# A gated scan with an expert for the top 128 rows: a re-planned instruction order, a rank counted on ScalarE from a second product, and fewer spare products

## The chip, the cores and the metric

The kernel runs on one core of one Trainium2 chip. The metric is the device time of one execution in microseconds; the median of three runs of the kernel before is 204.53 us (204.34 to 205.04).

## What is computed

Four sequences of 6208 tokens with 256 features go through a gated recurrence, and after it 128 tokens of each sequence go through a small expert network. In the reference, cut to what matters:

```python
sig = 1.0 / (1.0 + np.exp(-f_logit))
f = lower_bound + (1.0 - lower_bound) * sig
for t in range(S):                       # S = 6208
    h = f[:, t] * h + (1.0 - f[:, t]) * x[:, t]
    y[:, t] = h
...
scores = np.einsum('bsd,d->bs', y, w_gate)
for b in range(B):                       # B = 4
    top_idx = np.argpartition(-scores[b], capacity)[:capacity]   # capacity = 128
    xe = y[b, top_idx]
    ye = np.maximum(xe @ w1, 0.0) @ w2   # 256 -> 1024 -> 256
    g = 1.0 / (1.0 + np.exp(-scores[b, top_idx]))
    out[b, top_idx] = xe + g[:, None] * ye
```

All inputs and outputs are float32.

## The kernel before, in words

**Units.** The four sequences are cut into 25 units of at most 1024 tokens (UNITS, L27), six or seven to a sequence (a batch, in the code's words). Features lie on the partitions, in two halves. A unit is loaded as its gate logits and its x, each 1 MB, either by two transfers (L390) or, where two neighbouring buffers are free, by one of 2 MB (L393). ScalarE makes the gate (L396) and from it the factor of the scan (L400). POOL scales x (L404) and weighs it by the gate (L408); a share of the columns (SHARE, L28) is weighed by VectorE instead (L417). VectorE scans each half (L420). TensorE makes the scores of the tokens (L429) and turns the result so that tokens lie on the partitions (L373); ScalarE, or for the units in EASED (L29) VectorE, copies the turned blocks back (L444), and SP's queue stores the unit (L447). All buffers of a unit come from 22 slots of one tile, whole.

**Search.** When a sequence is scanned, choose() finds its 128 best tokens. The scores are spread over 32 lanes (L515), each lane gives its 16 best (L525 to L531, places by L527 and L540), 14 of these per lane are laid out as a row of 448 candidates, which one product broadcasts to all partitions (row(), L546, into the PSUM tile acc), and each partition ranks four candidates of its own against that row: it counts how many are greater. A rank is a counting pass of VectorE (L563), or, for the numbers in SIGNED, a sum of signs on ScalarE (L560, settled at L568). From each rank a 0/1 mark is made (L576) on POOL or VectorE, and four small products with the marks (pull(), L580) put the chosen token numbers in order on the partitions. The searches of batches 0 to 2 work in acc, one PSUM bank; that of batch 3 (RUSH) keeps its lanes in score, another bank, and its row in acc. A flag product (tell(), L593) follows, which says whether the result is complete.

**Expert.** POOL gathers the 128 rows from the output in HBM (fetch(), L650), so it comes after the stores that wrote them. TensorE turns the gathered rows (L674; L678 for batch 3), makes the up products (L720; L711), ScalarE the ReLU (L728), TensorE the down products (L733; L738), VectorE the sum with the gate (L745; L742), and POOL scatters the rows back (L749). For batches 0 and 1 the last two units are held: they stay in their slots, their stores come last of all in SP's queue, and the search's rows in them are picked by products. A tiny copy on POOL ("passed", L789) stands between the first held store and the other three, which wait for it in SP's queue. In batch 3 POOL touches each stored unit of that batch first (see(), L635), which makes it wait for the unit's store.

**What sets the order.** Nothing is left to a scheduler: a class Plan takes all steps with their costs and what they depend on, places them on the engines one by one, and the instructions are emitted in that order. The tables at the top of the file (SHARE, EASED, CAPS, SINGLE, FIND, EXPERT, EXTRA and others) are its settings: which unit takes which path, how far ahead loads go, when a search or an expert may start. Each engine then works through its own list in order, so whatever stands behind a waiting instruction waits too. SP's queue holds all loads and stores in one order. In gaps of TensorE the plan puts spare products (L962), and at the end L958, whose results nobody reads.

For a step that works in a search bank the plan keeps two times of that bank: a reader waits for the last writer, and a writer for the last reader.

Of the kernel before, what the change touches and what calls it, by code (L numbers as in the profile page):

```python
# [19 lines left out]
P = 128  # L20
# [7 lines left out]
SHARE = [2, 1, 1.75, 0.25, 0.5, 0, 0.5, 1, 0.375, 0.125, 1, 0.125, 0, 1, 0, 0, 1, 0.25, 1, 0.375, 0, 0.875, 0.875, 0.125, 0]  # L28
EASED = [0, 1, 2, 4, 6, 8, 9, 10, 15, 16, 18, 22, 23]  # L29
SLOTS = {"big": 22, "pt": 2, "gt": 2}  # L30
SCRATCH = 1024
CAPS = {"x": 30, "f": 3, "y": 17}
SINGLE = [2, 5, 8, 11, 17, 18, 24]
PAIR, PATIENCE, LONE = 4.915, 0, -2.5
APART = [2]
RUSH = [3]
SIGNED = [[], [2, 3], [2, 3], []]
XFER, FIRST = 2.485, 2.4
AHEAD, BACKLOG, STORE = 5, 4, 450
TURN, PUT, FIND, EXPERT = 22, 1, [-570, -1350, -705, -4710], [-85, -1920, -1020, -440]  # L40
WEIGHTS_AT = 8
EXTRA = [140, 140, 180, -120, 40, -160, 100, -160, -200, -120, -200, 120, 60, 0, -80, 80, -100, -140, 120, 0, 200, -140, 60, -40, -60]
# [6 lines left out]
KEEP, SPARE, SLACK, WAKE, COLD = 0.9, 0.11, 0.1, 2.0, 5.2  # L49
# [10 lines left out]
HEADS = -620  # L60
# [13 lines left out]
class Plan:  # L74
# [23 lines left out]
    def run(self):  # L98
# [17 lines left out]
        wrote, read = {}, {}  # L116
# [15 lines left out]
        def can(i):  # L132
            when = ready[i]
            for name, writes in self.bank[i]:
                when = max(when, (read if writes else wrote).get(name, 0.0))
# [26 lines left out]
        for done in range(n):  # L162
# [77 lines left out]
            for name, writes in self.bank[i]:  # L240
                last = wrote if writes else read
                last[name] = max(last.get(name, 0.0), end + HOP)
# [28 lines left out]
def gated_scan_moe(tc, xf, heads_in, lbwg, w12, outs, cap):  # L271
    nc = tc.nc
    v, a, pe, g = nc.vector, nc.scalar, nc.tensor, nc.gpsimd
    with ExitStack() as ctx:
# [214 lines left out]
        def choose(b):  # L489
# [8 lines left out]
            def chain(eng, cost, fn, key=None, extra=(), after=None, over=None, bank=()):  # L498
                key = key or ("search", b, len(plan.ops))
                add(eng, cost, fn, p0 + 0.01 * len(plan.ops), [after or last[0], *extra], key, load=2.0 if eng == "pe" else 1.0, over=over, bank=bank)  # L500
                last[0] = key
                return key
# [6 lines left out]
            bank = score[:, 1 - b % 2] if rush else acc  # L509
            own0 = NPOS + OWN if rush else A_OWN  # L510
# [36 lines left out]

            def own(what):
# [8 lines left out]
            def ranks(k):  # L557
                if k in SIGNED[b]:
                    junk = new("junks", [P, ROW], BF16)
                    a.activation(junk, acc[:, :ROW], ACTF.Sign, scale=-1.0, bias=st["mine"][:, k : k + 1], accum_out=st["sign"][:, k : k + 1])  # L560
# [12 lines left out]
            def marks(k):  # L573
                if k == 0:
                    st["hot"] = new("hot", [P, OWN, P], BF16)
                (v if rush and k in (SIGNED[b] or [OWN - 1]) else g).tensor_scalar(st["hot"][:, k], slot, st["rank"][:, k : k + 1], None, ALU.is_equal)  # L576
# [38 lines left out]
            ranked, s = [], r  # L615
# [408 lines left out]
```

## Time and profile before

| | us |
|---|---|
| median of 3 runs | 204.53 |
| lowest, highest | 204.34, 205.04 |
| the profiled execution | 204.95 |
| its span, first to last instruction | 202.8 |

| engine | busy us (share of the span) |
|---|---|
| TensorE products | 188.8 (93%) |
| VectorE | 160.8 (79%) |
| ScalarE | 154.3 (76%) |
| POOL | 150.4 (74%) |

The transfers move 79.64 MB, at 393 GB/s over the span. The span is what the profile's timelines cover; the execution's own time is a little more than 2 us longer. A share of busy time is a mean over the whole span: what limits a stretch is read from that stretch, in the windows, and from the waits ahead of an instruction, which a timeline row gives in square brackets with what ended them. TensorE's busy time contains the spare products.

### The profile page before, as it was taken

The numbers are of one execution on the slowest core, as the hardware profiler recorded it, in microseconds if no ns is written. First come the engines' busy times: TensorE is split into PE (matmuls) and PEld (weight loads), VectorE is DVE, ScalarE is ACT, GpSimd is POOL, SyncE is SP. The second block draws the span as 40 slices with busy tenths as digits, with TensorE's granted clock in tenths as the row PEclk, the third lists the DMA queues.
The fourth block names the chain that finished last, engine by engine and source line by source line (L and its number), as shares of the span: only waits on it lengthen the run. The fifth ranks groups of instructions, "written<-read, shape, count | busy, mean of one in ns | idle before, by whom it ended". The sixth has DMA issues, their size and how long they took to land. (4 is left out here: it accounts for less than half of the span.)

```text
span 202.8 us, 4152 instructions
## 1 busy us (share of the span) xinstructions
PE 188.8 (93%) x1613; PEld 138.8 (68%) x1613; DVE 160.8 (79%) x195; ACT 154.3 (76%) x201; POOL 150.4 (74%) x143
## 2 busy tenths in 40 slices
PE   5899999989898899999999999999999998999990
PEld 3677788666665677775975667766975756759890
DVE  1859896995999889999869899999999959591210
ACT  3788898798786995889999999986979988612210
POOL 6152899995776999997999998599868997233231
PEclk9999999999999999999999999999999999999997
DMA  6999999999999999999999999999999999996941
GB/s 198 402 434 436 409 399 434 417 419 436 422 422 419 417 441 423 425 430 430 422 415 425 423 402 375 300 445 414 436 419 415 423 430 427 420 420 247 430 175 36
DMA packets 9655, 79.64 MB, mean 393 GB/s; under 512 B 1313, under 2 KB 1581, under 8 KB 2720
## 3 DMA queue, kind: packets, MB, share of 16 engines
q1 hardware_dynamic: 9104, 78.39, 93.3%
q0 software_dynamic: 384, 0.95, 1.4%
q8 instruction: 14, 0.23, 0.4%
q14 instruction: 9, 0.07, 0.1%
q10 hardware_dynamic: 144, 0.00, 0.0%
HBM read 53.48 MB, written 25.95 MB: 392 GB/s over the span
## 5 line engine op out<-in xcount | busy, mean ns | idle before, releaser
L420 DVE TENSOR_TENSOR_SCAN whole<-gt,whole 128x1024 f32<-128x1024 f32 (+1 forms) x42 | 96.6, 2314 | 2.3 <-POOL whole L408 1.0
L408 POOL TENSOR_TENSOR whole<-whole 128x1024 f32<-128x1024 f32 (+6 forms) x41 | 84.8, 2084 | 6.8 <-ACT whole L396 5.5
L373 PEld LDWEIGHTS pt<-ident,whole 128*128 128x128 f32 x384 | 48.3, 196 | 21.9 <-ACT whole L444 10.4
L373 PE MATMUL pt<-ident,whole 128*128 128x128 f32 x384 | 59.8, 293 | 2.4 <-ACT whole L444 2.3
L400 ACT ACTIVATE gt<-whole,nl 128x1024 f32<-128x1024 f32 (+2 forms) x50 | 54.6, 1097 | 6.8 <-DVE whole L420 5.5
L404 POOL TENSOR_SCALAR whole<-whole,nl 128x1024 f32<-128x1024 f32 (+6 forms) x41 | 41.0, 1011 | 19.0 <-DMA whole<-xf 13.6
L444 ACT COPY whole<-pt 128x512 f32<-128x512 f32 (+1 forms) x86 | 47.3, 590 | 8.3 <-PE pt L373 7.1
L396 ACT ACTIVATE whole<-whole 128x2048 f32<-128x2048 f32 (+2 forms) x25 | 46.3, 1855 | 6.2 <-DMA whole<-xf 6.0
L962 PE MATMUL score<-slot,ones 128*128 128x256 bf16 x356 | 48.2, 282 | 2.4 <-POOL slot L305 1.9
L962 PEld LDWEIGHTS <-ones 128*128 128x128 bf16 x356 | 35.4, 102 | 10.0 <-issue 4.0
L429 PE MATMUL score<-whole,wgr 128*32 128x256 f32 x384 | 32.3, 391 | 1.4 <-DVE whole L420 0.9
L417 DVE SCALAR_TENSOR_TENSOR whole<-gt,whole 128x1024 f32<-128x1024 f32 (+6 forms) x19 | 15.5, 818 | 8.8 <-ACT gt L400 8.7
L420 DVE TENSOR_TENSOR_SCAN whole<-gt,tl,whole 128x1024 f32<-128x1024 f32 (+1 forms) x8 | 15.3, 1933 | 0.1
L429 PEld LDWEIGHTS score<-whole,wgr 128*32 128x32 f32 x384 | 8.2, 108 | 9.2 <-DVE whole L420 3.4
L666 PE MATMUL acc<-whole,hT 128*128 128x256 f32 x64 | 14.5, 379 | 0.0
L576 POOL TENSOR_SCALAR hot<-slot,rank 128x128 bf16<-128x128 bf16 x15 | 9.0, 607 | 6.1 <-DVE vals L571 5.4
L666 PEld LDWEIGHTS acc<-whole,hT 128*128 128x128 f32 x64 | 11.9, 190 | 1.4
L720 PE MATMUL pm<-xT,wt 128*128 128x128 f32 x96 | 11.8, 279 | 0.0
L720 PEld LDWEIGHTS pm<-xT,wt 128*128 128x128 f32 x96 | 11.1, 192 | 0.5 <-ACT xT L691 0.5
L749 POOL DMA_INDIRECT out<-res,aim x4 | 4.1, 1034 | 9.5 <-DVE xT L684 4.6
L728 ACT ACTIVATE hT<-pm 128x512 f32<-128x512 f32 x8 | 4.7, 590 | 6.0 <-PE pm L711 2.4
L563 DVE TENSOR_SCALAR_CACHE_REDUCE junk<-acc,mine 128x448 bf16<-128x448 f32 x12 | 8.1, 678 | 1.2 <-ACT junks L560 0.8
(124 smaller groups left out, 131.9 us busy)
## 6 DMA issues: line engine op xcount, KB each, us to landing
whole<-xf SPq DMA_DIRECT2D x16, 2048.0 KB, 18.3
out<-whole SPq DMA_DIRECT2D x23, 1024.0 KB, 14.2
whole<-xf SPq DMA_DIRECT2D x14, 1024.0 KB, 21.8
wt<-w SPq DMA_DIRECT2D x1, 2048.0 KB, 25.5
whole<-xf SPq DMA_DIRECT2D x2, 768.0 KB, 7.7
out<-whole SPq DMA_DIRECT2D x1, 768.0 KB, 12.6
tl<-heads SPq DMA_DIRECT2D x1, 512.0 KB, 3.7
whole<-xf SPq DMA_DIRECT2D x2, 256.0 KB, 4.1
```

Source lines behind the costliest of these rows:

```text
L373: pe.transpose(out, src, ident)
L396: a.activation(fs[i], fs[i], ACTF.Sigmoid, scale=-1.0)
L400: a.activation(gs[i, h][:, :n], fs[i][:, h], ACTF.Identity, scale=nl[:, h : h + 1], bias=1.0)
L404: g.tensor_scalar(xs[i][:, h, c0:], xs[i][:, h, c0:], nl[:, h : h + 1], 1.0, ALU.mult, ALU.mult)
L408: g.tensor_tensor(xs[i][:, h, c0:], xs[i][:, h, c0:], fs[i][:, h, c0:], ALU.mult)
L417: v.scalar_tensor_tensor(xs[i][:, h, :c1], gs[i, h][:, :c1], 1.0, xs[i][:, h, :c1], ALU.subtract, ALU.mult)
L420: v.tensor_tensor_scan(xs[i][:, h], gs[i, h][:, :n], xs[i][:, h], carry[h] if blk0 else tl[:, 1, h, b, TAIL - 1 : TAIL], ALU.mult, ALU.add ...
L429: pe.matmul(score[j * CG : (j + 1) * CG, b % 2, c0:], wgr[:, h, CG - 1 - r : 2 * CG - 1 - r], src, start=(h == 0 and blk0 + q < 3), stop=( ...
L444: (v.tensor_copy if eng == "dve" else a.copy)(out, src)
L666: pe.matmul(acc[:, :D], st["hits"][:, c], yms[last_unit[b] - k][:, c], start=(k == 0 and c == 0), stop=(k == HELD[b] - 1 and c == NF - 1))
L720: pe.matmul(st["pm", f // TP][:, c : c + P], w1t[:, h, f * P : (f + 1) * P], st["xT"][:, h], start=(h == 0), stop=(h == NH - 1))
L962: pe.matmul(score[:, h].rearrange("p (k c) -> p k c", k=2), ones, slot.unsqueeze(1).to_broadcast([P, 2, P]), start=not begun, stop=True, s ...
```

## The change

The change has four parts.

1. **The plan's account of a search bank.** Of each bank the plan now keeps, per engine, the time of its last access of either kind, and a step waits for every other engine's last access; an engine's own earlier steps don't hold it up.
2. **The last search.** SIGNED for batch 3 becomes [3]: the fourth rank is counted by ScalarE, not VectorE. It reads a second copy of the row of candidates, made by a second product (row_aside) into a PSUM buffer of the class gt, so another bank. The marks of the last two ranks are made on VectorE (swift), those of the first two on POOL. In batch 1 one rank less is ScalarE's.
3. **"passed" moves.** The tiny copy that releases three of the held stores now comes ahead of batch 3's gather, which depends on it; before, it came behind.
4. **The tables.** KEEP goes from 0.9 to 0.8 and SLACK from 0.1 to 0.2, which govern the spare products (306 are emitted, 356 before), and all other settings of the plan are replaced. So every engine's list is in another order.

Of the tables two lines stand for all:

```diff
-EASED = [0, 1, 2, 4, 6, 8, 9, 10, 15, 16, 18, 22, 23]
+EASED = [1, 3, 4, 5, 14, 21, 23, 24]
-SIGNED = [[], [2, 3], [2, 3], []]
+SIGNED = [[], [3], [2, 3], [3]]
...
-KEEP, SPARE, SLACK, WAKE, COLD = 0.9, 0.11, 0.1, 2.0, 5.2
+KEEP, SPARE, SLACK, WAKE, COLD = 0.8, 0.11, 0.2, 2.0, 5.2
...
-        wrote, read = {}, {}
+        touched = {}
...
-                when = max(when, (read if writes else wrote).get(name, 0.0))
+                when = max([when, *(t for who, t in touched.get(name, {}).items() if who != self.ops[i][0])])
...
             for name, writes in self.bank[i]:
-                last = wrote if writes else read
-                last[name] = max(last.get(name, 0.0), end + HOP)
+                touched.setdefault(name, {})[e] = end + HOP
...
+            swift = [OWN - 2, OWN - 1] if rush and SIGNED[b] else [OWN - 1] if rush else []
...
+            def row_aside():
+                st["aside"] = hold(("aside",), [P, 4 * BLK], "aside")
+                pe.matmul(st["aside"][:, :ROW], onesf[:LANE], st["diag"].rearrange("p l e -> p (l e)"), start=True, stop=True)
...
-                    a.activation(junk, acc[:, :ROW], ACTF.Sign, scale=-1.0, bias=st["mine"][:, k : k + 1], accum_out=st["sign"][:, k : k + 1])
+                    a.activation(junk, (st["aside"] if rush else acc)[:, :ROW], ACTF.Sign, scale=-1.0, bias=st["mine"][:, k : k + 1], accum_out=st["sign"][:, k : k + 1])
...
-                (v if rush and k in (SIGNED[b] or [OWN - 1]) else g).tensor_scalar(st["hot"][:, k], slot, st["rank"][:, k : k + 1], None, ALU.is_equal)
+                (v if k in swift else g).tensor_scalar(st["hot"][:, k], slot, st["rank"][:, k : k + 1], None, ALU.is_equal)
...
-            ranked, s = [], r
+            s = r
+            if rush and SIGNED[b]:
+                s = chain("pe", 1.01, row_aside, after=r, over=0.09, takes=[("aside",)])
+                plan.tile(("aside",), ("gt", "gt"), [("aside", "read")])
             for k in range(OWN):
                 if k in SIGNED[b]:
-                    s = chain("act", 0.74, lambda k=k: ranks(k), after=s, extra=[m], bank="acc r")
+                    s = chain("act", 0.74, lambda k=k: ranks(k), ("aside", "read") if rush else None, after=s, extra=[m], bank=() if rush else "acc r")
                     continue
                 r = chain("dve", 0.65, lambda k=k: ranks(k), after=r, extra=[m], bank="acc r")
-                quick = rush and not SIGNED[b] and k == OWN - 1
+                quick = k in swift
                 marked.append(chain("dve" if quick else "pool", 0.25 if quick else 0.605, lambda k=k: marks(k), after=r))
             if SIGNED[b]:
-                r = chain("act", 0.2 * len(SIGNED[b]), settle, after=s, extra=[r])
-                marked += [chain("dve" if rush else "pool", 0.25 if rush else 0.605, lambda k=k: marks(k), after=r) for k in SIGNED[b]]
+                r = chain("act", 0.2 * len(SIGNED[b]), settle, after=s, extra=[] if rush else [r])
+                marked += [chain("dve" if k in swift else "pool", 0.25 if k in swift else 0.605, lambda k=k: marks(k), after=r) for k in SIGNED[b]]
...
-            add("pool", 1.1, fetch, p0, [("st", b), ("index", b), ("seen", N - 2) if halved else None, ("store", last_unit[b] - HELD[b]), ("store", "tail", b)], k("fetch"))
+            ahead = [("st", b), ("index", b), ("seen", N - 2) if halved else None, ("store", last_unit[b] - HELD[b]), ("store", "tail", b)]
+            if halved and len(stored) > len(unheld) + 1:
+                first = stored[len(unheld) + 1]
+                add("pool", 0.12, lambda: g.tensor_copy(yms[first][:1, 0, :1], yms[first][:1, 0, :1]), p0, ahead, ("passed",))
+                ahead = [*ahead, ("passed",)]
+            add("pool", 1.1, fetch, p0, ahead, k("fetch"))
...
-                if len(stored) > len(unheld) + 1:
-                    first = stored[len(unheld) + 1]
-                    add("pool", 0.12, lambda: g.tensor_copy(yms[first][:1, 0, :1], yms[first][:1, 0, :1]), p0 - 2, [k("fetch")], ("passed",))
```

POOL at the end of the program, before: the copy of the indices of batch 3, the six touches of stored units (L635), the gather of batch 3 (xe_109 is the tile that takes its rows) and the tiny copy "passed" (L789).

```order
L638 COPY index<-idx 128x1 [waits DVE_49]
L635 MEMSET whole 1x1 [waits DMAHW0_49]
L635 MEMSET tl 1x1 [waits DMAHW3_49,Pool_49]
L635 MEMSET whole 1x1 [waits DMAHW1_49]
L635 MEMSET whole 1x1 [waits DMAHW2_49]
L635 MEMSET whole 1x1 [waits DMAHW3_49]
L635 MEMSET whole 1x1 [waits DMAHW4_49,Activation_49]
L650 DMA xe_109<-out,idx 128x256 [waits DMAHW5_49]
L789 COPY whole<-whole 1x1
L749 DMA out<-res,aim 6208x256 [waits DMASW2_49,DVE_49]
```

The same place in the new order, with the numbers of the new file:

```order
L645 COPY index<-idx 128x1 [waits DVE_49]
L642 MEMSET whole 1x1 [waits DMAHW1_49]
L642 MEMSET tl 1x1 [waits Pool_49]
L642 MEMSET whole 1x1 [waits DMAHW2_49]
L642 MEMSET whole 1x1 [waits DMAHW3_49]
L642 MEMSET whole 1x1 [waits DMAHW4_49]
L642 MEMSET whole 1x1 [waits DMAHW5_49,Activation_49]
L779 COPY whole<-whole 1x1
L657 DMA xe_109<-out,idx 128x256 [waits DMAHW6_49]
L756 DMA out<-res,aim 6208x256 [waits DMASW2_49,DVE_49]
```

The tiny copy (now L779) stands ahead of the gather and has no wait of its own; the wait for the store of the last unit (a DMAHW semaphore) stands on the gather alone.

TensorE from the last of the four products of batch 3's pull (L580) on, before: L720 and L733 are batch 2's up and down products, L593 is the flag, L678 turns the rows of batch 3's gather (xe_109). Four more up products of batch 2 (L720, x4) stand ahead of the pull.

```order
L580 LDWEIGHTS hot
L580 MATMUL acc<-vals,hot 128x3
L720 MATMUL pm<-xT,wt 128x128 x4
L593 LDWEIGHTS ones
L593 MATMUL acc<-bad,ones 128x1
L720 MATMUL pm<-xT,wt 128x128 x8
L733 MATMUL py<-wt,hT 128x256 x8
L678 MATMUL pm<-ident,xe_109 128x128 x2
```

And now, with the numbers of the new file (L584 is the pull, L967 a spare product, L597 the flag, L727 and L740 are the up and down products):

```order
L584 LDWEIGHTS hot
L584 MATMUL acc<-vals,hot 128x3
L967 LDWEIGHTS ones
L967 MATMUL warm<-slot,ones 128x512
L597 LDWEIGHTS ones
L597 MATMUL acc<-bad,ones 128x1
L727 MATMUL pm<-xT,wt 128x128 x16
L740 MATMUL py<-wt,hT 128x256 x8
L967 LDWEIGHTS ones
L967 MATMUL warm<-slot,ones 128x512
```

All 16 up products of batch 2 stand behind the pull and the flag now. Behind the last row shown come two more spare products, and then the turn of batch 3's rows (L685).

VectorE in the search of batch 3, before, from the places of each lane's second eight to the pulled number (L563 are the ranks, L700 is the gate product of batch 2's expert, L576 a mark):

```order
L540 MAX_INDEX at<-ci,rest 32x8
L543 CAST ci<-at 32x16
L563 TENSOR_SCALAR junk,rank<-acc,mine 128x448
L571 TENSOR_SCALAR vals<-score 128x4
L563 TENSOR_SCALAR junk,rank<-acc,mine 128x448 x2
L700 SCALAR_TENSOR_TENSOR res,gate<-xe_107,wgrow 128x256
L563 TENSOR_SCALAR junk,rank<-acc,mine 128x448
L576 TENSOR_SCALAR hot<-slot,rank 128x128
L585 TENSOR_REDUCE idx<-acc 128x1
```

And now (L443 is the copy of a turned block, L567 a rank, L580 a mark, L707 the gate product):

```order
L540 MAX_INDEX at<-ci,rest 32x8
L443 COPY whole<-pt 128x4x128
L543 CAST ci<-at 32x16
L567 TENSOR_SCALAR junk,rank<-acc,mine 128x448 x2
L575 TENSOR_SCALAR vals<-score 128x4
L567 TENSOR_SCALAR junk,rank<-acc,mine 128x448
L580 TENSOR_SCALAR hot<-slot,rank 128x128 x2
L707 SCALAR_TENSOR_TENSOR res,gate<-xe_107,wgrow 128x256
L589 TENSOR_REDUCE idx<-acc 128x1
```

One rank has gone, a copy has come in ahead of the ranks, a second mark has come, and the gate product stands behind the marks.

## Rows read from the trace of the kernel before

**Rows 1.** The page's first line.

```profile
span 202.8 us, 4152 instructions
```

**Rows 2.** Windows: stretch us, each engine's busy us (instructions), granted clock, DMA share, GB/s.

```profile
120.00:125.00 5.00, 4.82 (x49) 3.31 (x48) 4.90 (x9) 5.00 (x9) 4.23 (x6) 1.00 1.01 387
...
125.00:130.00 5.00, 4.96 (x44) 3.80 (x43) 4.75 (x7) 5.00 (x10) 4.57 (x4) 1.00 1.02 326
...
175.00:180.00 5.00, 4.94 (x51) 2.62 (x50) 3.45 (x15) 1.66 (x3) 0.01 (x1) 1.00 1.00 415
...
184.50:185.00 0.50, 0.50 (x7) 0.50 (x7) 0.00 (x0) 0.00 (x0) 0.50 (x1) 1.00 0.16 66
```

**Rows 3.** Timeline of VectorE: start us, us, engine, line, what [idle before].

```profile
170.81 2.35 DVE L420 TENSOR_TENSOR_SCAN whole<-gt,whole 128x1024 f32<-128x1024 f32 x1 [0.30 <-ACT gt L400]
...
179.19 0.68 DVE L563 TENSOR_SCALAR_CACHE_REDUCE junk<-acc,mine 128x448 bf16<-128x448 f32 x1 [0.32 <-PE acc L546]
...
181.25 0.42 DVE L700 SCALAR_TENSOR_TENSOR res<-xe,wgrow 128x256 f32<-128x256 f32 x1
...
181.60 0.68 DVE L563 TENSOR_SCALAR_CACHE_REDUCE junk<-acc,mine 128x448 bf16<-128x448 f32 x1
...
182.32 0.25 DVE L576 TENSOR_SCALAR hot<-slot,rank 128x128 bf16<-128x128 bf16 x1
...
182.93 0.15 DVE L590 TENSOR_SCALAR bad<-acc 128x1 bf16<-128x1 f32 x1
```

**Rows 4.** Timeline of TensorE, products and the last weight load.

```profile
179.16 1.47 PE L958 MATMUL warm<-slot,ones 128*128 128x512 bf16 x6
...
181.31 1.16 PE L720 MATMUL pm<-xT,wt 128*128 128x128 f32 x8
...
182.34 0.47 PE L580 MATMUL acc<-vals,hot 128*128 128x3 bf16 x4
...
183.68 2.03 PE L720 MATMUL pm<-xT,wt 128*128 128x128 f32 x16
...
185.54 3.62 PE L733 MATMUL py<-wt,hT 128*128 128x256 f32 x16
...
188.78 0.36 PEld L678 LDWEIGHTS pm<-ident,xe 128*128 128x128 f32 x2
```

**Rows 5.** Timeline of POOL.

```profile
184.15 1.11 POOL L650 DMA_INDIRECT xe<-out,idx  x1 [0.52 <-issue]
...
185.26 0.18 POOL L789 COPY whole<-whole 1x1 f32<-1x1 f32 x1
...
198.06 0.99 POOL L749 DMA_INDIRECT out<-res,aim  x1 [1.51 <-POOLq L874]
```

**Rows 6.** Line L650, gathers of batches 1, 2 and 3: issue to landing.

```profile
DMA to landing us min/median/max: 8.9/8.9/8.9
DMA to landing us min/median/max: 6.6/6.6/6.6
DMA to landing us min/median/max: 3.3/3.3/3.3
```

**Rows 7.** Groups by line and form: times, busy us, mean ns.

```profile
L417 DVE SCALAR_TENSOR_TENSOR whole<-gt,whole 128x1024 f32<-128x1024 f32 x6 | 7.3, 1218 | 2.9 <-ACT gt L400 2.9
...
L444 DVE COPY whole<-pt 128x512 f32<-128x512 f32 x11 | 7.4, 674 | 0.2 <-PE pt L373 0.2
```

**Rows 8.** Waits: engine, line, waited for, us in total, times, longest.

```profile
DVE mine L555 <- PE acc L546: 1.3, 1, 1.3
...
DVE junk L563 <- ACT junks L560: 0.8, 1, 0.8
```

**Rows 9.** Line L447, the store of batch 3's last unit.

```profile
L447 SPq DMA_DIRECT2D out<-whole x1: 332/332/332, 177.3 to 177.3; - x1
...
DMA to landing us min/median/max: 6.2/6.2/6.2
```

**Rows 10.** Line L962, the spare products.

```profile
L962 PE MATMUL score<-slot,ones x356: 269/273/421, 1.9 to 169.4; 128*128 128x256 bf16 x178
```

More of the change, by code (lines that the diff above doesn't have):

```diff
@@ L27 @@
 UNITS = [[1, 3, 4, 4, 4, 4, 4], [4] * 6, [4] * 6, [4] * 6]
-SHARE = [2, 1, 1.75, 0.25, 0.5, 0, 0.5, 1, 0.375, 0.125, 1, 0.125, 0, 1, 0, 0, 1, 0.25, 1, 0.375, 0, 0.875, 0.875, 0.125, 0]
-EASED = [0, 1, 2, 4, 6, 8, 9, 10, 15, 16, 18, 22, 23]
+SHARE = [2, 2, 1.625, 0, 0.875, 0.625, 0.875, 0, 0.625, 0, 1, 0.5, 0.375, 1, 0.125, 0, 0.25, 0.875, 0.375, 1, 1, 0, 0.875, 0.375, 0.5]
+EASED = [1, 3, 4, 5, 14, 21, 23, 24]
 SLOTS = {"big": 22, "pt": 2, "gt": 2}
 SCRATCH = 1024
-CAPS = {"x": 30, "f": 3, "y": 17}
-SINGLE = [2, 5, 8, 11, 17, 18, 24]
-PAIR, PATIENCE, LONE = 4.915, 0, -2.5
+CAPS = {"x": 33, "f": 3, "y": 21}
+SINGLE = [2, 10, 11, 13, 16, 18, 19, 21]
+PAIR, PATIENCE, LONE = 4.915, 8.5, 10.5
 APART = [2]
 RUSH = [3]
-SIGNED = [[], [2, 3], [2, 3], []]
+SIGNED = [[], [3], [2, 3], [3]]
 XFER, FIRST = 2.485, 2.4
[L39 to L42, printed above, removed]
+AHEAD, BACKLOG, STORE = 15, 3, 320
+TURN, PUT, FIND, EXPERT = 12, -13, [-3450, -405, -4655, -8840], [-1005, -2245, -985, 175]
+WEIGHTS_AT = 6
+EXTRA = [-60, 200, -40, -100, 200, -200, -60, 60, 120, 200, -60, -80, 0, 60, 40, -80, -200, 80, -80, 0, -140, 160, -20, 140, 80]
 AFTER = "pull"
@@ L59 @@
 HALF = 2048
-HEADS = -620
+HEADS = -860
 NROW = NBLK // 4 + 1
@@ L496, in choose, with chain @@
             last = [None]
-            def chain(eng, cost, fn, key=None, extra=(), after=None, over=None, bank=()):
+            def chain(eng, cost, fn, key=None, extra=(), after=None, over=None, bank=(), takes=()):
                 key = key or ("search", b, len(plan.ops))
-                add(eng, cost, fn, p0 + 0.01 * len(plan.ops), [after or last[0], *extra], key, load=2.0 if eng == "pe" else 1.0, over=over, bank=bank)
+                add(eng, cost, fn, p0 + 0.01 * len(plan.ops), [after or last[0], *extra], key, load=2.0 if eng == "pe" else 1.0, over=over, bank=bank, takes=takes)
                 last[0] = key
```

## The prediction

> **What bounds the kernel now.** The page's first line gives the span of the profiled execution, 202.8 us [rows 1]; the execution itself took 204.95 us, so 2.15 us lie around the span. The median of the runs shown is 204.53, that is 0.42 below the profiled one. I make the sum against 204.95 and take 0.42 off at the end. Read next the windows [rows 2]: in the last third the share of the DMA engines stays at 1.0 (387, 326 and 415 GB/s) and VectorE is busy for 4.90 and 4.75 of 5 us. So until the last scan two things are full, the queue of transfers and VectorE. In 184.50 to 185.00 the share is 0.16: here the queue runs dry before its stores are done.
>
> From VectorE's timeline [rows 3] take the anchor S: the last scan starts at 170.81, lasts 2.35 and ends at S = 173.16. Behind S stands a chain. The search of batch 3 makes its ranks (179.19 to 182.32) and the marks, and TensorE pulls the indices out, from 182.34 for 0.47, done at 182.81 [rows 4]. Then TensorE does the rest of batch 2's expert, up to 185.71 and down from 185.54 for 3.62, and only then, at 188.78, it turns the rows of batch 3's gather. POOL issued that gather at 184.15 [rows 5], and it landed 3.3 us later [rows 6], at 187.4. So the gather waited 1.3 us for TensorE. From 188.78 to the end of the span are 14.0 us, the expert of batch 3, its scatter and the landing; the change leaves these steps as they are. The question is when TensorE takes up that turn (T, now 188.78): it needs its own queue done and the gather landed.
>
> **The change part by part.** *The order up to S.* SP's order has before the last load the same 10 MB of unit stores as now, only other ones, and one tail store more (64 KB, under 0.2 us at 415 GB/s). So the last load lands where it does now, and nothing that moves among loads and stores gives time at the end. On VectorE I count what stands between the first maximum of batch 1's search and the last scan, in both orders: one rank more (0.68 [rows 3]), eight products for seven, with 768 elements more (1.22 per 1024 [rows 7], so 0.9), two copies of turned blocks fewer (0.67 each [rows 7]); together +0.3. Against that stand the stalls of the searches in the shared bank, 1.3 and 0.8 us in the search of batch 2 [rows 8]: the new plan counts a bank as taken by one engine at a time, so it can put other work there. All of it gone gives S = 171.4, none gone 173.5; an estimate for the search of batch 1 is that 0.8 more goes there, the size of the smaller of the two, so 170.6 is the early end. I take S = 171.9, since VectorE needs its rows in order behind ScalarE and POOL in any plan and I see no reason for either end. That is 1.3 us early.
>
> *The search of batch 3.* The fourth rank leaves VectorE: its 0.72 (181.60 to 182.32 [rows 3]) go. The gate product of batch 2, which starts at 181.25 and holds the fourth rank up by 0.35, moves behind the marks: another 0.35. One mark more runs on VectorE, 0.25. In its place a copy of a turned block (0.67 [rows 7]) stands ahead of the first rank, which had 0.32 us of idle time to give [rows 3], so +0.35. The second row product (its twin took 1.01 us of TensorE) and ScalarE's count lie beside VectorE's three ranks; if that cover were gone, the third mark would wait up to 1.0 us. Sum -0.5: the pull is done at S + 9.15 instead of S + 9.65, that is at 181.05.
>
> *TensorE between the pull and T.* Now 5.97 us (182.81 to 188.78). In the new order the first quarter of batch 2's up products no longer stands ahead of the pull, and nothing but a spare product fills the wait for the flag. So behind the pull come: the flag's inputs and its product, 0.65 (VectorE ends the flag's input at 183.08, 0.27 after the pull [rows 3], and the product with its hops follows); the up products, 1.16 for the first 8 of 32 passes, as much for the next 8 and 2.03 for the last 16 [rows 4], 4.35; the down products 3.62; three spare products, 0.25 each by the six in 1.47 [rows 4], 0.74. That is 9.36, or 3.4 us more. TensorE is free at 181.05 + 9.36 = 190.4, which is S + 18.5. What cost nothing before, because the wait for the flag was filled, is now on the path.
>
> *The gather of batch 3.* It reads rows that the stores of batch 3 write, so POOL waits for the last of them. That store is issued at 177.3 and lands 6.2 us later [rows 9], at 183.5. The new queue has the same bytes ahead of it, so it lands at 183.5 again, and the gather starts at about 183.7, 0.45 earlier than now; a faster search cannot pull it further. So the whole gain of the search ends at this landing. More important is what lies beside the gather. Now the tiny copy that releases the last three held stores stands behind it (185.26, after 184.15 [rows 5]), and the queue is nearly empty meanwhile (0.16 [rows 2]). In the new order that copy stands ahead of it and does not wait for the last store, so the three stores are in the queue before the gather is. A gather into the idle queue took 3.3 us to land, the two into a full one shown took 6.6 and 8.9 [rows 6]. I take 6.6, because it also ran beside 1 MB stores: 183.7 + 6.6 = 190.3.
>
> The Trainium skill ("DMA: Bandwidth & Descriptors", on queues, rings and completion order) says that each DMA engine goes round the queues packet by packet and empties a packet of some 9 to 17 descriptors before it changes over. That speaks against this edit, and the rows agree with it in sign: 3.3 us more in a full queue. An estimate from that page: 9 to 17 packets of 8 KB ahead on each of 16 engines, at the measured 415 GB/s 0.31 us each, are 2.8 to 5.3 us on top of 3.3, so the gather would land at 189.8 to 192.3 and T would be 190.4 to 192.3, against the 190.4 that the rows give.
>
> *The rest.* The held stores now run on without the gap, so they end earlier by that stretch; the scatters that wait for them are off the path, since the last scatter (198.06) stood 1.51 us idle for the mix [rows 5]. Nothing is gained there.
>
> **The sum.** T is the later of 190.4 (TensorE) and 190.3 (gather): 190.4, or 1.6 us later than 188.78. The span becomes 204.4, the profiled execution 206.55, and less 0.42 this is 206.1 us. Two causes that don't depend on each other give nearly the same T, so either alone is enough.
>
> **Rivals.** *Faster: the queue runs ahead.* From 120 to 130 us it moved 387 and 326 GB/s at a full share [rows 2], against 415 later. At 415 the same bytes are through 1.4 us earlier. If that slow stretch doesn't return in the new order, the last store lands at 182.1 and the gather, still beside stores, at 188.9; S, which follows the loads, can come to its early end less 1.4, 169.2, and TensorE is free at 169.2 + 18.5 = 187.7. With the gather then a little better than 6.6, at 5.5 (between the ends), T is 187.8, 1.0 us early: 203.5. It decides from T < 188.2. For it: the slow rows lie where one gather (the one of 8.9) ran, and that gather moves. Against it: three gains must meet.
>
> *No change: the queues interleave.* If the gather's transfers are taken in turn with the stores', it hardly feels them. By the 3.3 of [rows 6] the gather then lands at 187.0, and TensorE alone sets T: with S at 170.6, 170.6 + 18.5 = 189.1, 0.3 late, 204.8. Against it stand the 6.6 and 8.9. The Trainium skill says in the same page (issuing engines are not separate DMA queues) that the transfers of all issuing engines interleave on the same 16 DMA engines, which speaks for it.
>
> *That it doesn't do what it says*: ScalarE's count could wait for the second product and end behind VectorE's third rank; then the search keeps its length, the pull is at S + 9.65 and T at 190.9, 206.6. Within the forecast's range.
>
> *Slower still: TensorE's clock.* It is granted 1.00 in all these windows [rows 2], the upper of its two levels (2.4 GHz). The spare products that fill its gaps fall from 356 [rows 10] to 306. If a gap now lets the grant fall to 1.2 GHz before the experts, the products between pull and T (7.97 of the 9.36 us) slow down in that stretch. No row holds a product at the lower level, so I bound it by the ratio of the two: a quarter of them at twice the time is 2 us, 208.1.
>
> **How the numbers follow.** Forecast, T between 189.5 and 191.5 (205.2 to 207.2): 0.52. Faster rival: 0.27, since nearly every edit of the order can also shorten waits that I don't see. Interleaved or in between, T within 0.6 of now: 0.15. Clock or S at its late end (173.5, so T = 192.0, 207.7): 0.06. About 0.3% (0.6 us) is what a measurement of this kernel can tell from no change. So faster 0.27, same 0.15, slower 0.58. The range is 203.4 (the faster rival) to 207.3 (the forecast's late end); outside it I leave the clock and a deeper gain.
>
> **What would show it.** In the new profile the last scan should end near 171.9, the pull near 181.0, the gather should start near 183.7 with the DMA share at 1.0 beside it and land near 190.3; TensorE should go from the flag through 32 up and 16 down products without a stop and turn batch 3's rows at 190.4. If the gather lands under 4 us after its start, the term of the full queue was wrong. If TensorE stands idle before the turn by more than 1 us, S came earlier than I took it and the gather alone sets the time. If the last store of batch 3 lands before 182, the queue ran ahead, and the faster rival holds.

## The result, and the profile after

The changed kernel takes 207.57 us (median of four runs, 207.37 to 208.07), the kernel before beside it 204.78. The ratio is 1.011, with a 95% interval of 1.007 to 1.015: slower, as forecast. The forecast was 206.1 in a range of 203.4 to 207.3. Applied to the 204.53 from which it was made, the ratio gives 206.8, inside the range; the median of 207.57 itself lies 0.3 above its upper end. The profiled execution took 207.37, where the sum had 206.55. Every ratio here and below leaves out executions that lie over 1.5% above the fastest of the same kernel.

The span, which answers to [rows 1]:

```profile
span 205.5 us, 4047 instructions
```

The windows of the changed kernel, with the columns of [rows 2] (each engine's busy us, granted clock, DMA share, GB/s):

```profile
120.00:125.00 5.00, 4.60 (x42) 2.96 (x39) 4.80 (x4) 5.00 (x7) 4.79 (x4) 1.00 1.05 418
125.00:130.00 5.00, 5.00 (x34) 3.88 (x31) 4.90 (x3) 4.75 (x6) 4.92 (x4) 1.00 0.97 407
...
185.00:190.00 5.00, 0.31 (x2) 0.00 (x0) 0.26 (x1) 0.00 (x0) 1.03 (x1) 1.00 0.96 395
190.00:195.00 5.00, 4.89 (x27) 4.45 (x28) 0.69 (x4) 1.03 (x3) 1.70 (x2) 0.66 0.18 66
```

Three things are new. The slow stretch of the queue (387 and 326 GB/s in [rows 2]) is not there. From 185 to 190 no engine works for more than 1.03 us while the queue is nearly full: everything waits for a transfer. And from 190 to 195 TensorE is granted only 0.66 of its clock on average (by single us 0.50 from 191 to 193, the lower of its two levels, 1.2 GHz, and 1.00 again from 194).

VectorE (start us, us, engine, line, what), which answers to [rows 3]:

```profile
163.71 4.58 DVE L419 TENSOR_TENSOR_SCAN whole<-gt,whole 128x1024 f32<-128x1024 f32 x2
...
176.37 0.41 DVE L580 TENSOR_SCALAR hot<-slot,rank 128x128 bf16<-128x128 bf16 x2
```

The last scan ends at 163.71 + 4.58 = 168.29, 4.9 us earlier than the 173.16 of before, and 3.6 earlier than forecast. At the first maximum of batch 1's search 2.3 of these 4.9 us are there already; the two rows are of the kernel before and of the changed one:

```profile
106.34 0.36 DVE L525 MAX8 ci<-acc 32x8 f32<-32x194 f32 x1 [1.58 <-PE acc L515]
```

```profile
104.04 0.35 DVE L525 MAX8 ci<-acc 32x8 f32<-32x194 f32 x1 [1.20 <-PE acc L515]
```

TensorE, which answers to [rows 4]:

```profile
176.50 0.54 PE L584 MATMUL acc<-vals,hot 128*128 128x3 bf16 x4
...
177.39 3.82 PE L727 MATMUL pm<-xT,wt 128*128 128x128 f32 x32
181.04 3.62 PE L740 MATMUL py<-wt,hT 128*128 128x256 f32 x16
184.50 0.81 PE L967 MATMUL warm<-slot,ones 128*128 128x512 bf16 x3
190.11 0.41 PE L685 MATMUL pm<-ident,xe 128*128 128x128 f32 x2 [4.81 <-DMA xe<-out,idx]
...
190.82 5.31 PE L718 MATMUL pm<-xT,wt 128*128 128x128 f32 x32
```

TensorE has done all of batch 2 at 185.31 and then stands idle for 4.81 us, for the gather. It turns batch 3's rows at 190.11 (forecast 190.4), and the 32 up products behind that take 5.31 us, where the same 32 took 3.84 in the kernel before. POOL, and the time of its gather, which answer to [rows 5, 6]:

```profile
179.86 0.17 POOL L779 COPY whole<-whole 1x1 f32<-1x1 f32 x1
182.56 1.10 POOL L657 DMA_INDIRECT xe<-out,idx  x1 [2.52 <-DMA out<-whole]
...
DMA to landing us min/median/max: 7.4/7.4/7.4
```

The tiny copy lets the held stores go at 179.86. The gather waits until 182.56 for the last store of batch 3 and lands 7.4 us later, at 190.0, instead of 3.3.

### The profile page after: what moved, and what is told of

It reads as the page before. It is cut to its first block, busy times and chain, and to the rows that moved or that the text cites. A ratio compares the mean times of both kernels' runs of the same rounds, so it can differ in the third digit from the quotient of the medians.

```text
span 205.5 us, 4047 instructions
## 1 busy us (share of the span) xinstructions
PE 183.3 (89%) x1561; PEld 136.8 (67%) x1561; DVE 161.0 (78%) x194; ACT 155.8 (76%) x205; POOL 142.0 (69%) x142
## 5 line engine op out<-in xcount | busy, mean ns | idle before, releaser
L407 POOL TENSOR_TENSOR whole<-whole 128x1024 f32<-128x1024 f32 (+6 forms) x41 | 79.3, 1949 | 8.0 <-ACT whole L395 7.7
L372 PE MATMUL pt<-ident,whole 128*128 128x128 f32 x384 | 58.8, 291 | 3.5 <-ACT whole L443 2.9
L443 ACT COPY whole<-pt 128x512 f32<-128x512 f32 (+1 forms) x90 | 49.2, 588 | 9.6 <-PE pt L372 9.5
L403 POOL TENSOR_SCALAR whole<-whole,nl 128x1024 f32<-128x1024 f32 (+6 forms) x41 | 38.8, 954 | 21.8 <-DMA whole<-xf 21.7
L971 PE MATMUL score<-slot,ones 128*128 128x256 bf16 x306 | 41.0, 284 | 1.9 <-POOL slot L304 1.9
L971 PEld LDWEIGHTS <-ones 128*128 128x128 bf16 x306 | 30.8, 102 | 8.1 <-issue 2.5
L428 PE MATMUL score<-whole,wgr 128*32 128x256 f32 x384 | 31.3, 390 | 4.8 <-DVE whole L419 4.0
L416 DVE SCALAR_TENSOR_TENSOR whole<-gt,whole 128x1024 f32<-128x1024 f32 (+7 forms) x21 | 18.4, 875 | 3.7 <-ACT gt L399 3.7
L428 PEld LDWEIGHTS score<-whole,wgr 128*32 128x32 f32 x384 | 8.8, 108 | 13.4 <-DVE whole L419 7.8
L580 POOL TENSOR_SCALAR hot<-slot,rank 128x128 bf16<-128x128 bf16 x14 | 8.4, 605 | 5.6 <-DVE junk L567 5.4
L727 PE MATMUL pm<-xT,wt 128*128 128x128 f32 x96 | 11.5, 278 | 0.0
L727 PEld LDWEIGHTS pm<-xT,wt 128*128 128x128 f32 x96 | 11.0, 192 | 0.4 <-ACT open L711 0.4
L567 DVE TENSOR_SCALAR_CACHE_REDUCE junk<-acc,mine 128x448 bf16<-128x448 f32 x12 | 8.0, 665 | 0.2 <-PE acc L546 0.2
```

The costliest lines, as they stand in the source:

```text
L372: pe.transpose(out, src, ident)
L403: g.tensor_scalar(xs[i][:, h, c0:], xs[i][:, h, c0:], nl[:, h : h + 1], 1.0, ALU.mult, ALU.mult)
L407: g.tensor_tensor(xs[i][:, h, c0:], xs[i][:, h, c0:], fs[i][:, h, c0:], ALU.mult)
L416: v.scalar_tensor_tensor(xs[i][:, h, :c1], gs[i, h][:, :c1], 1.0, xs[i][:, h, :c1], ALU.subtract, ALU.mult)
L428: pe.matmul(score[j * CG : (j + 1) * CG, b % 2, c0:], wgr[:, h, CG - 1 - r : 2 * CG - 1 - r], src, start=(h == 0 and blk0 + q < 3), stop=( ...
L443: (v.tensor_copy if eng == "dve" else a.copy)(out, src)
```

## The experiments

Each run starts from the kernel before or from the changed kernel and names what differs. The kernel before took 204.5 to 204.6 us beside all of them.

### The gather and the copy

**The changed kernel with the copy behind the gather again** (after_gather_first). On POOL two instructions change places, and TensorE has one spare product less ahead of the turn of batch 3's rows; all other lists are the same. POOL's list, in short:

```diff
-L779 COPY whole<-whole 1x1
 L657 DMA xe<-out,idx 128x256
+L796 COPY whole<-whole 1x1
```

> The changed kernel with only its third part undone: the tiny copy that releases three held stores stands behind batch 3's gather again; the lists of all engines are otherwise those of the changed kernel. Theory 1 (the gather was late because the released stores were in the queue beside it, and the expert behind it then ran at a lower clock): the gather starts at 182.6 as now but lands 3.3 us later instead of 7.4, at about 185.9; TensorE, free at 185.3, waits less than 1 us instead of 4.8, keeps its clock at 1.00, and the 32 up products take 3.84 us instead of 5.31. That is 4.0 + 1.5 us less than 207.57: 202.1 (201.5 to 203.0), below both kernels. Theory 2 (the gather's 7.4 us belong to the place and time of the gather in the new order, not to the copy): the landing stays near 190 and the time at 207.4. Theory 3 (the gain is given back, because the held stores then end later and their scatters set the end): gather at 185.9, but the end stays above 204.

203.63 us, ratio to the kernel before 0.994 (0.991 to 0.997); so 3.9 us less than the changed kernel, from one exchanged pair of instructions. The first profile fence is TensorE's timeline, the second POOL's with the gather's time to landing:

```profile
186.19 0.41 PE L685 MATMUL pm<-ident,xe 128*128 128x128 f32 x2 [0.34 <-DMA xe<-out,idx]
...
186.90 3.84 PE L718 MATMUL pm<-xT,wt 128*128 128x128 f32 x32
```

```profile
183.08 1.10 POOL L657 DMA_INDIRECT xe<-out,idx  x1 [2.61 <-DMA out<-whole]
184.19 0.18 POOL L796 COPY whole<-whole 1x1 f32<-1x1 f32 x1
...
196.30 0.98 POOL L756 DMA_INDIRECT out<-res,aim  x1 [5.60 <-DMA out<-whole]
197.59 0.99 POOL L756 DMA_INDIRECT out<-res,aim  x1 [0.30 <-DMA out<-res,aim]
...
DMA to landing us min/median/max: 3.0/3.0/3.0
```

Theory 1 holds for the gather (3.0 us), the wait (0.34) and the up products (3.84 again). Theory 3 holds for a part: the expected 202.1 was missed by 1.5 us. From the turn to the end of the span are 15.6 us, not 14.0 as before. The rows of POOL say why: a scatter at 196.30 waited 5.60 us for a held store, and batch 3's scatter, whose rows were ready at 194.76, stood behind it.

**That, with batch 3's scatter ahead of batch 1's** (gather_first_scatters_swapped). Of the line that gives a scatter its conditions only the last one changes, which is shown here:

```diff
-*([("moe", c, "scatter") for c in range(b) if HELD[c]] if halved else [])
+*([("moe", 0, "scatter")] if halved else [("moe", B - 1, "scatter")] if b == 1 else [])
```

> The run after_gather_first with one more edit: on POOL the scatter of batch 3 stands ahead of the scatter of batch 1, which waits for the last held store; all other lists are the same. In the trace of after_gather_first batch 1's scatter starts at 196.30, 0.8 after the last held store landed, and batch 3's, whose rows are mixed at 194.76, stands behind it and starts at 197.59. Theory 1 (part of the gain is given back at the end, because the scatters stand in POOL's list behind the held stores): batch 3's scatter starts 0.5 after its mix, at 195.3, batch 1's at 196.6, and the end comes 1.0 us earlier: 202.6 (202.0 to 203.2). Theory 2 (the end hangs on the landing of the held stores alone, or the two scatters only change places): 203.6.

202.22 us, ratio 0.9875 (0.985 to 0.990). POOL's two last scatters:

```profile
194.88 0.98 POOL L756 DMA_INDIRECT out<-res,aim  x1 [4.33 <-DVE res L749]
196.18 1.00 POOL L756 DMA_INDIRECT out<-res,aim  x1 [0.30 <-issue]
```

Batch 3's scatter now follows its own mix, and the last one starts 1.4 us earlier; the time is 1.4 us less. Theory 1 holds, and this kernel has the lowest median of all (the best kernel, in what follows): 1.25% below the kernel before, 2.6% below the changed one.

**The kernel before with the copy ahead of the gather** (before_copy_first). Again two instructions of POOL change places and nothing else.

> The kernel before with only the third part of the change: the tiny copy stands ahead of batch 3's gather. Theory 1: the gather starts near 184.3 as it does in the kernel before, but beside three stores, and lands 6.6 to 7.4 us later, at 191 to 191.7 instead of 187.4; TensorE, free at 188.8, waits 2.2 to 2.9 us; the time is 204.8 + 2.2 to 2.9, so 207.0 to 207.7, and up to 1.5 more if the clock falls during the wait. Theory 2 (the long landing belongs to the new order): landing after 3.3 us, the time within 0.5 of 204.8.

205.64 us (median of all twelve executions), ratio 1.0046 (1.0015 to 1.0076). TensorE, and the gather's time to landing:

```profile
191.25 0.41 PE L678 MATMUL pm<-ident,xe 128*128 128x128 f32 x2 [2.69 <-DMA xe<-out,idx]
...
191.96 3.84 PE L711 MATMUL pm<-xT,wt 128*128 128x128 f32 x32
```

```profile
DMA to landing us min/median/max: 6.3/6.3/6.3
```

In the one execution with a trace the mechanism is there in the old order too: 6.3 us for 3.3, and TensorE waits 2.69. The size was missed. The profiled execution took 207.47, as expected, but the eleven executions that the ratio counts lie from 205.02 to 207.90 with a median of 205.54, only 0.9 us above the kernel before; a twelfth took 210.56. How long the gather took in the shorter runs no trace shows; that stays open.

**One held store more ahead of the gather** (after_two_stores_behind): as after_gather_first, but the copy stands ahead of the last two held stores instead of the last three.

> The run after_gather_first with one held store more let go ahead of batch 3's gather, so two of the four held stores stand ahead of it and two behind; all other lists are the same. Theory 1 (the gather's lateness is set by the stores in the queue at its issue and beside it): it starts at 183.0 and lands between the 3.0 us of after_gather_first and the 7.4 us of the changed kernel, near 187.7; TensorE waits about 2 us; T is 187.9, and since the queue runs less dry the held stores end earlier than in after_gather_first, before batch 3's rows are mixed at 196.5: 204.0 to 205.0. Rival (one store beside it is enough for the whole delay): landing near 190, 206 to 207.5.

204.06 us, ratio 0.997 (0.994 to 0.9996). The gather's time to landing, and TensorE:

```profile
DMA to landing us min/median/max: 5.1/5.1/5.1
```

```profile
188.71 0.41 PE L685 MATMUL pm<-ident,xe 128*128 128x128 f32 x2 [1.86 <-DMA xe<-out,idx]
...
189.42 3.84 PE L718 MATMUL pm<-xT,wt 128*128 128x128 f32 x32
```

So the gather takes 3.0 us with none of the three stores let go ahead of it, 5.1 with one and 7.4 with all three. One is not enough for the whole delay; theory 1 holds. Little else differs between these three kernels, so the time of the gather follows the stores let go ahead of it.

### The clock

**Spare products in TensorE's wait** (after_warm_wait, and once more beside a repeated run of the changed kernel, after_repeated and after_warm_wait_repeated). One number changes, and 17 more spare products stand ahead of the turn:

```diff
-LAND = [6.0, 6.0, 6.0, 1.85]
+LAND = [6.0, 6.0, 6.0, 6.0]
```

> The changed kernel with one number changed: the plan takes the landing of batch 3's gather as 6.0 us instead of 1.85 us after its issue, and so it puts about 17 more spare products on TensorE ahead of the turn of batch 3's rows; no other engine's list changes. They fill about 4.2 of the 4.8 us in which TensorE stands idle. Theory 1 (idle time lets the grant fall, and that costs 1.5 us): the granted clock stays at 1.00 from 190 to 195 and the 32 up products of batch 3 take 3.84 us instead of 5.31: 207.57 - 1.47 = 206.1 (205.8 to 206.5). Rival (the up products are slowed by the stores and scatters beside them, not by the clock; or the clock falls whatever TensorE does before): they stay near 5.3 and the time at 207.3 to 207.9.

> The changed kernel once more, as the measure for the next run, with which it shares the chip: 207.4 (207.0 to 208.0), TensorE idle for 4 to 5 us ahead of batch 3's rows, clock 0.6 to 0.7 behind that, the 32 up products in 5.2 to 5.4 us. If its gather lands at another time than 190.0, the time moves with it.

> The run after_warm_wait once more, since its runs lay far apart (205.89 to 208.84): 17 spare products in TensorE's wait for the gather. Theory 1 (the fall of the clock costs the difference of the up products, 5.3 against 3.84): 1.0 to 1.6 us below the changed kernel of the same chip. Rival (the spare products' work gives the same time back elsewhere, for instance by a later landing of the gather): within 0.4 of it.

The first pair was not clear: 207.05 us (205.89 to 208.84) against 207.57, where 206.1 was expected. The second, on one chip: the changed kernel 208.17 (ratio 1.017, 1.012 to 1.021; just above its expected 207.0 to 208.0), with the spare products 206.75 (1.011, 1.006 to 1.017), 1.4 us apart though their intervals overlap. By their times alone the gain is likely, not shown. The traces are clear on the clock. TensorE and a window of the repeated changed kernel, then the same of the run with spare products:

```profile
190.39 0.66 PE L685 MATMUL pm<-ident,xe 128*128 128x128 f32 x2 [5.02 <-DMA xe<-out,idx]
...
191.27 4.77 PE L718 MATMUL pm<-xT,wt 128*128 128x128 f32 x32
```

```profile
190.00:195.00 5.00, 4.61 (x28) 4.17 (x29) 0.69 (x4) 1.06 (x3) 1.16 (x2) 0.67 0.13 52
```

```profile
184.86 4.48 PE L967 MATMUL warm<-slot,ones 128*128 128x512 bf16 x20
190.44 0.41 PE L685 MATMUL pm<-ident,xe 128*128 128x128 f32 x2 [1.10 <-DMA xe<-out,idx]
...
191.15 3.84 PE L718 MATMUL pm<-xT,wt 128*128 128x128 f32 x32
```

```profile
190.00:195.00 5.00, 4.48 (x37) 4.12 (x38) 0.69 (x4) 1.06 (x3) 1.37 (x2) 1.00 0.14 57
```

The turn comes at the same time (190.4), but with the wait filled the grant stays at 1.00 and the products take 3.84 us, not 4.77. That is 0.9 us of the 1.4; the spans of the two traces are 1.0 apart. The rival that the stores beside them slow the products falls, since the stores are there in both (DMA share 0.13 and 0.14). In the first pair's trace a part of the gain was covered by a gather that landed later (8.1 us after its issue, the turn at 191.03 and not 190.11).

### The search and the plan

**All four ranks on VectorE** (after_rank_on_vector, from the changed kernel; swapped_rank_on_vector, from the best one): the last list in SIGNED is empty again.

> The changed kernel with only its second part undone in batch 3: all four ranks of the last search on VectorE, no second copy of the row, one mark on VectorE and three on POOL. Everything ahead of that search is the same. Theory 1 (since TensorE waits 4.8 us for the gather, and the gather for the last store of batch 3, the length of the search is hidden): the pull ends 0.4 to 0.9 us later than 177.0, the gather lands within 0.3 of 190.0, and the time stays within 0.4 of 207.57. Rival (the search is on the path): 0.4 to 0.9 us longer, 208.0 to 208.5.

> The run gather_first_scatters_swapped with the second part of the change undone in batch 3: all four ranks of the last search on VectorE. There TensorE takes up batch 3's rows as soon as its own queue is done, so the length of the search is no longer covered by a wait for the gather. From the traces of after_rank_on_vector and of the changed kernel: the pull ends 9.7 us after the last scan with four ranks on VectorE and 8.75 with one on ScalarE, but TensorE is free 16.9 us after the last scan in the first and 17.0 in the second, since the waiting time ahead of the later pull is filled with up products of batch 2. Theory 1 (ScalarE's rank shortens the search and gives nothing, because TensorE's work for batch 2 fills the same time): 202.2, within 0.4. Rival (the search is on the path once the gather is early): 0.9 later, 203.1.

207.85 us against 207.57 (208.17 when repeated), and 202.53 against 202.22: 0.3 us each, less than these runs can tell from no change. In the first the wait for the gather covers the search. In the second nothing does, and its TensorE shows why it still costs no more:

```profile
178.49 0.71 PE L727 MATMUL pm<-xT,wt 128*128 128x128 f32 x4
179.04 0.24 PE L584 MATMUL acc<-vals,hot 128*128 128x3 bf16 x4
179.15 1.14 PE L727 MATMUL pm<-xT,wt 128*128 128x128 f32 x8
...
180.15 2.48 PE L727 MATMUL pm<-xT,wt 128*128 128x128 f32 x20
...
186.13 0.38 PE L685 MATMUL pm<-ident,xe 128*128 128x128 f32 x2
```

The pull ends at 179.28, 9.7 us after the last scan (165.02 + 4.57), against 8.8 with ScalarE's rank. But of the 32 up products four are done ahead of the pull and eight in the wait for the flag, there is one spare product less, and TensorE turns batch 3's rows at 186.13; with ScalarE's rank it was 186.07. The search became 0.9 us shorter and gave nothing.

**The account of a search bank, alone** (before_bank_account: the kernel before with the new account and its old tables; after_old_account: the changed kernel with the old account).

> The kernel before with the first part of the change alone: the plan's account of a search bank, with all tables as before; the plan then orders every engine anew. Theory 1 (the account itself takes the stalls of the shared bank away): the waits of VectorE in the search of batch 2, 1.3 and 0.8 us, are gone and the last scan ends up to 2 us earlier, near 171.2; since the gather still lands near 187.4, T comes at most 1.2 earlier: 203.4 to 204.6. Theory 2 (the 4.9 us by which the last scan of the changed kernel ends earlier come from the tables): stalls as before or others, the last scan at 172.5 or later, 204.4 to 207.

> The changed kernel with only the plan's account of a search bank as it was before; the plan then orders every engine anew. Theory 1 (the account takes the stalls away): VectorE waits 1 to 2 us more in the searches of the shared bank and the last scan ends 1 to 2 us later than 168.3; TensorE's wait of 4.8 us for the gather shrinks by as much, and the time stays at 207.0 to 208.0. Theory 2 (the tables): the last scan ends within 0.7 of 168.3 and VectorE's waits are no longer than in the changed kernel.

203.16 us, ratio 0.994 (0.990 to 0.998), and 209.89, ratio 1.022 (1.017 to 1.028). So the account is worth 1.4 us by itself and 2.3 in the changed kernel (1.7 against its repeated run). Since with it the plan orders every engine anew, these are the prices of one order each. VectorE's last scan in the first and in the second:

```profile
168.66 2.34 DVE L419 TENSOR_TENSOR_SCAN whole<-gt,whole 128x1024 f32<-128x1024 f32 x1
```

```profile
169.97 2.35 DVE L420 TENSOR_TENSOR_SCAN whole<-gt,whole 128x1024 f32<-128x1024 f32 x1 [0.48 <-ACT gt L400]
```

It ends at 171.00 in the first, 2.2 earlier than before, and at 172.32 in the second, 4.0 later than in the changed kernel. In the first, theory 1 holds in its size (171.2 expected, and a time just below its range), but not in its list of stalls: VectorE's waits still have one of the two of [rows 8] and lack the other, so what gave the rest of the 2.2 us is not shown.

```profile
DVE mine L554 <- PE acc L545: 1.3, 1, 1.3
```

In the second the scan was to come 1 to 2 us later and the time to stay; it lost more than the wait for the gather could cover: batch 3's last store came later, the gather started at 185.15 and TensorE turned the rows at 192.55.

**The old settings of the spare products** (swapped_old_spares), from the best kernel: KEEP 0.9 and SLACK 0.1, 366 spare products for 306.

> The run gather_first_scatters_swapped with the settings of the spare products as before (KEEP 0.9, SLACK 0.1), so some 60 more spare products on TensorE; no other engine's list changes. Theory 1 (the number of spare products matters neither for the clock nor for the path): the clock is 1.00 in the same windows, 202.2 within 0.5. Rival (the spare products hold up TensorE's turns and scores, and so the stores, or fewer of them let the clock fall somewhere): over 0.5 off, either way.

202.99 us (202.09 to 204.08), ratio 0.992 (0.989 to 0.9955). The profiled execution has the shortest span of all traces (200.2), but the median is 0.8 above the best kernel's, with overlapping intervals. By the 0.5 of the expectation that is the rival's case, but the two were measured on different chips. Whether fewer spare products are worth a few tenths stays open. From 185 to 195 the clock is 1.00 with 306 as with 366.

## Why the prediction was right, and where it was wrong

**The anchor S: wrong.** Forecast 171.9, range 170.6 to 173.5; measured 168.29. The step that failed is the term of VectorE's stalls, where I took 1.6 us off and added 0.3, and the counting began only at the first maximum of batch 1's search, as if nothing ahead of it moved. Three things were left out. First, the time ahead of that maximum: it starts at 104.04 and not 106.34, and by the middles of ten traces of the new order and two of the old one it comes 1.7 us earlier; the counted stretch behind it became 2.2 shorter, inside the forecast's range for it. Second, what a new order gives beyond the stalls that the waits list by name: with the account alone, one of the two stalls remained and S was still 2.2 early. Third, S moves between runs of one order. In nine further traces whose lists up to there are the changed kernel's or differ by spare products only, it ended from 168.35 to 170.04, and for the old order 173.16 became 172.56 in before_copy_first. So the order gave some 3.6 us of the 4.9 (172.86 to 169.24, by the middles), the rest is the run. The slow stretch of [rows 2] was partly the run's as well: with the same lists before_copy_first moved 385 GB/s there, where the kernel before had 326.

**The search: right in kind, the gain too small.** Forecast 9.15 us from S to the end of the pull (9.65 before), measured 8.75.

**TensorE from the pull to its free moment: right in kind, too large.** Forecast 9.36, measured 8.27 (177.04 to 185.31). The wait for the flag took 0.35 instead of 0.65, and the up products, in one piece of 32, 3.65 until the down products start instead of 4.35 summed from pieces. With S this made TensorE free at 185.3 and not at 190.4. The sentence that two causes give nearly the same T, and either is enough, was wrong for this one.

**The gather: right, and it alone set the time.** Forecast: start 183.7, 6.6 us to landing, 190.3. Measured: 182.56, 7.4, 190.0. That the copy ahead of the gather is its cause is shown by after_gather_first, where that pair is exchanged and one spare product less is all that differs besides. The Trainium skill ("DMA: Bandwidth & Descriptors", on queues, rings and completion order) says that an engine empties a packet of descriptors of one queue before it turns to the next; by that page's figures the estimate was 2.8 to 5.3 us on top of 3.3 (it takes each 8 KB packet of a store for one of the page's descriptors). With three stores ahead the gather took 4.4 us more than the 3.0 of after_gather_first, inside that estimate; with one 2.1, below it.

What the gather waits for can be read from the DMA queues of before_copy_first. From its issue at 184.78 to 189.3 no packet of POOL's queue starts, while SP's queue moves 1.71 MB; from 189.3 to 190.3 the gather's 0.13 MB go, and SP's queue still moves 0.80 MB from 190.3 to 192.5. In after_gather_first all its packets go between 184.8 and 185.8, from 1.8 us after the issue on. So the gather waits for a part of the stores let in ahead of it, not for all of them; a queue that simply works through all bytes in order is not what this trace shows.

**From T to the end: wrong.** I kept the 14.0 us of before. Measured are 15.4 (190.11 to 205.5), and the 1.47 by which batch 3's up products are longer (5.31 for 3.84) covers the difference. The clock was among the rivals, but with 0.06, and for the products between pull and T; the wait that made it fall is the one that the gather itself caused, and it hit the products behind T. A forecast that lets a wait of several us arise has to carry that.

**The number: in part luck.** T came out at 190.1 for 190.4 although TensorE was free 5 us earlier than forecast, only because the gather alone sets it. The gather's own two errors cancel, a start 1.1 us early and a landing 0.8 longer; its 6.6 was the smaller of two rows from gathers elsewhere in the kernel. The end then took 1.4 us more, and around the span lay 1.9 us for 2.15: 206.55 - 0.3 + 1.4 - 0.3 = 207.4.

**The rivals.** The faster one had its first two conditions met: the queue ran ahead (last store of batch 3 at 182.3, forecast 182.1 for that case) and S came early. It fell by the gather. The rival of no change, a gather that hardly feels the stores, is refuted by the 5.1 and 7.4. That ScalarE's count comes late was not seen: the two marks on VectorE at 176.37 start without a wait.

Where the 2.8 us come from, by the runs:

| step | us | ratio to before |
|---|---|---|
| kernel before | 204.5 | 1 |
| with the new account of a bank alone | 203.2 | 0.994 |
| all of the change but the copy's new place | 203.6 | 0.994 |
| the changed kernel | 207.6 | 1.011 |
| all but the copy's place, last scatters exchanged | 202.2 | 0.9875 |

The first, second and fourth part together are no better than the first alone, because batch 3's scatter then stands behind batch 1's; with that pair exchanged they are.

## What to carry to other kernels

A small transfer on which the end of the program waits should be issued before large ones are let into the queues, even where the queue then runs dry for a moment: here a queue at 0.46 of its share for 5 us (180 to 185 in after_gather_first) cost some 1.4 us at the end, which exchanging two scatters gave back, and the late gather 3.9 net of that. An instruction that costs 0.17 us can carry such a release, so in a new order look at what each tiny step lets go, and ahead of whom. And a gain on the path before a wait is only worth what the wait lets through: look first at which wait would end last, then shorten the work ahead of it.

## What the runs showed of the hardware

- The time of one gather of 128 rows grew with the 1 MB stores let go ahead of it: 3.0, 5.1 and 7.4 us for none, one and three (6.3 to 8.1 for three, over all traces). Its first packet started 1.8 us after its issue with none ahead (after_gather_first) and 4.6 us with three (before_copy_first), where 0.80 MB of the stores still went behind it.
- After waits of TensorE of 1.9 and 2.7 us the granted clock stayed at 1.00. After 4.2 to 5.0 us (four traces) it had read 1.00 through most of the wait, fell to 0.50, the lower of its two levels (1.2 GHz), within about 0.6 us of the work's return, and stayed there for some 3 to 7 us; 32 up products took 4.77 to 6.29 us for 3.84. With spare products in the wait and 0.9 to 1.1 us left of it, it stayed at 1.00.
- With nearly the same lists, the last scan ended at times 1.75 us apart in ten traces. The whole time of the changed kernel varied by 1.4 over ten runs.
